# Clustered attention and a gated FFN on one core: masks of the last pairs written by VectorE, raw weights loaded two chunks ahead, results stored by quarters

## The chip, the cores and the metric

The kernel runs on one NeuronCore of a Trainium2 chip. The time is the device time of one execution in microseconds (us). Beside it stands the span of a profiled execution, which is what the views of the profile add up to.

## What is computed

Attention within clusters, for 4 batches, 8 heads, 768 tokens and 64 features, followed by a two-layer network with a hard-swish gate. Cut to what matters:

```python
q_assign = np.argmax(np.einsum('bhsd,hcd->bhsc', q_n, c_n), axis=-1)   # 16 clusters
k_assign = np.argmax(np.einsum('bhsd,hcd->bhsc', k_n, c_n), axis=-1)
mask = q_assign[:, :, :, None] == k_assign[:, :, None, :]
scores = np.where(mask, scale * np.matmul(q, k.transpose(0, 1, 3, 2)), -1e9)
attn = softmax(scores);  attn_out = np.matmul(attn, v)
x = attn_out.transpose(0, 2, 1, 3).reshape(3072, 512)
h = x @ w_in                          # 512 x 2048
g = h * np.clip(h + 3.0, 0.0, 6.0) / 6.0
out = g @ w_out                       # 2048 x 512
```

The weights w_in and w_out arrive as 64-bit floats, so the kernel has to make 32-bit floats of them itself.

## The kernel before, in words

**Steps.** Two heads are worked on together as a pair; there are 16 pairs. A pair has 12 steps (two halves of 384 queries, six chunks of 128 keys), so there are 192 steps, numbered n, and r = n mod 12 is the place in the pair. In a step, `scores` computes the scores of both heads into a PSUM tile `ps` (two such tiles exist), `exponentials` has ScalarE write exp of them into `ex`, `key_sums` has GpSimd add `ex` to a running sum `acc`, and `attn_v` multiplies `ex` by v into `pv`. When a half is done, `divide` multiplies `acc` by ones on TensorE (`pd`), VectorE takes the reciprocal `rcp` and multiplies it into `num`, and `num` is stored to a scratch tensor `xd` in DRAM.

**The mask.** A score of different clusters must vanish. `route` finds each token's cluster as a one-hot row; `route_turn` transposes the rows on TensorE (`po`) and ScalarE copies them to `xm`, scaled by -2^60 for keys (whose one-hot is inverted). In `scores_part`, a bf16 product of `xm` adds -2^60 to the scores of unlike clusters, and an f32 product of `xf` (the transposed q and k) adds the scores. The names `MASKED`, `by_vector`, `masks`, `clusters` and `spread` belong to another way, in which VectorE masks `ex` with cluster numbers; with `MASKED = NPAIR` no pair uses it.

**Preparing a pair.** `prep_items` spreads the work for the next pair over the steps: `turn` (12 transpositions `pqk` of q and k, copied to `xf`), `cluster_scores` (`pcs`), `route`, `route_turn`.

**Weights.** `decoding_steps` gives five steps for each of 32 chunks of 64-bit weights (`raw`, two buffers): `split`, `join`, `power`, `rest`, `total`, on VectorE and ScalarE. `split` of chunk i also issues the load of chunk i+1. `share` says how many of these steps follow each pair of scores steps. After the chunks, `weight_sums` and `make_first_sums` form sums of weights on VectorE.

**The network.** It is computed by a scheme with seven products in place of eight (half-size blocks, sums before and after). A block of 256 tokens is 15 items: eight `up` (products `uX`, `uY`, VectorE's sums `sx` and `g_sb`, ScalarE's `lift`, VectorE's `clip`, GpSimd's gated sums) and seven parts of `down` (products `X` and `Y`, sums into `y0` and `y1`). There are twelve blocks. `psum_m`, two banks, holds the outputs of both.

**Order.** The order on every engine is written out by hand in the recording loop; each engine runs its instructions in that order, and semaphores hold one that depends on another engine. Up to step 96 (`DECODED`) steps come two at a time. From there `four_by_four` groups them: at r mod 4 = 0 a block of scores, then `attn_v` of four steps; at r mod 4 = 2 a block of scores and after it the fill, some four items of the network with the next pair's preparation between them. After step 192 only the network is left. Nearly all DMAs are issued by SyncE (SP), which too waits in order.

**Lines of the profile.** L418 is the scores product (`ps`), L441 exp, L461 and L464 `acc`, L474 `pv`, L495 `pd`, L499 and L500 `rcp` and `num`, L310 `pqk`, L323 `pcs`, L367 `po`, L208 the load of raw weights, L221 to L252 the decoding, L658 and L669 the up products and sums, L693 and L700 the down products and sums, L740 and L742 the stores of results.

Of the kernel before, what the change touches and what calls it, by code (L numbers as in the profile page):

```python
# [116 lines left out]
def fast_path(ctx, tc, ok, q, k, v, centroids, moe_w_in, moe_w_out, out):  # L117
# [26 lines left out]
    rawp = decoding.enter_context(tc.tile_pool(name="rawp", bufs=2))  # L144
# [24 lines left out]
    MASKED = NPAIR  # L169
# [40 lines left out]
    def decoding_steps(i):  # L210

        got = {}

        def split():
            load_weights(i + 1)
            raw = st.pop(("raw", i))
            got.update(lo=raw[:, :, 0], hi=raw[:, :, 1])
            got["size"] = decp.tile([P, WC], BF16, name="wsize")
            got["top"] = psum_t.tile([P, WC], U32, name="wtop", tag="t")
            got["unit"] = decp.tile([P, WC], U32, name="wunit")  # L220
            nc.scalar.activation(  # L221
                out=got["size"], in_=got["hi"].bitcast(F32), func=ACT.Abs,
                accum_out=w_totals[:, 0, i : i + 1],
            )
            nc.vector.tensor_scalar(
                out=got["top"], in0=got["hi"], scalar1=3, scalar2=0x3FFFFFFF,
                op0=ALU.logical_shift_left, op1=ALU.bitwise_and,
            )

        def join():  # L230
            nc.vector.scalar_tensor_tensor(
                out=got["top"], in0=got["hi"], scalar=0xC0000000, in1=got["top"],
                op0=ALU.bitwise_and, op1=ALU.bitwise_or,
            )

        def power():
            nc.scalar.activation(
                out=got["size"], in_=got["size"], func=ACT.Relu, bias=w_low, scale=-1.0,
                accum_out=w_totals[:, 1, i : i + 1],
            )  # L240
            nc.vector.tensor_scalar(
                out=got["unit"], in0=got["top"], scalar1=0xFF800000, scalar2=None, op0=ALU.bitwise_and
            )

        def rest():
            unit = got["unit"].bitcast(F32)
            nc.vector.scalar_tensor_tensor(
                out=unit, in0=got["lo"], scalar=2.0**-52, in1=unit, op0=ALU.mult, op1=ALU.mult
            )

        def total():
            nc.vector.tensor_tensor(  # L252
                out=chunks[i][0], in0=got["top"].bitcast(F32), in1=got["unit"].bitcast(F32), op=ALU.add
            )

        return [split, join, power, rest, total]
# [6 lines left out]
    number = const.tile([P, C], BF16, name="number")  # L263

    def constants():
        make_identity(nc, ident)
        for t in range(2):
            nc.vector.tensor_reduce(
                out=parity[:, t : t + 1],
                in_=ident.rearrange("p (h t c) -> p t h c", t=2, c=C)[:, t], axis=AX.XY, op=ALU.max,  # L270
            )
        nc.gpsimd.memset(half_c, 0.5)
        nc.gpsimd.memset(low_c, 1.0 / BOUND)
        nc.gpsimd.memset(ones, 1.0)
        nc.gpsimd.memset(w_low, W_LOW)
        nc.gpsimd.memset(one_hot, 0.0)
        for c in range(C):
            nc.gpsimd.memset(number[:, c : c + 1], float(c))

        warm = psum_t.tile([P, 4, P], F32, name="warm", tag="t")  # L280
        for i in range(14):
            nc.tensor.transpose(out=warm[:, i % 4], in_=ident, identity=ident)
# [11 lines left out]
    def centroid_turn():  # L294
        pc = scratch([P, P], "pc")
        nc.tensor.transpose(out=pc, in_=st.pop("wide"), identity=ident)
        nc.vector.tensor_copy(out=cnT, in_=pc)
# [5 lines left out]
    def turn(g, part):  # L303
# [4 lines left out]
        for i in range(4):  # L308
            j = part * 4 + i
            nc.tensor.transpose(out=pt[:, i], in_=qk[:, j // NCH, j % NCH], identity=ident)  # L310
        dst = xf[:, part * 4 : part * 4 + 4]
        nc.scalar.copy(out=dst, in_=pt)
# [17 lines left out]
    def route(g):  # L330
# [27 lines left out]
        if g >= MASKED:  # L358
            numbers.append(lambda: clusters(g))

    def route_turn(g, part):
# [7 lines left out]
        nc.scalar.activation(out=dst, in_=po, func=ACT.Copy, scale=-FAR if part else 1.0)  # L369
# [6 lines left out]
    def clusters(g):  # L376
        oh = one_hot.rearrange("p j (t c) -> p j t c", t=2)[:, :, :, 0:C]
        which = rtp.tile([P, NC2, 2, C], BF16, name="which")
        nc.vector.tensor_tensor(
            out=which, in0=oh, in1=number.unsqueeze(1).unsqueeze(1).to_broadcast([P, NC2, 2, C]), op=ALU.mult  # L380
        )
        qid = st["qid"] = rtp.tile([P, NCH, 2], BF16, name="qid")
        kid = st["kid", g] = kidp.tile([P, NCH, 2], F32, name="kid")
        nc.vector.tensor_reduce(out=kid, in_=which[:, NCH:], axis=AX.X, op=ALU.add)

        nc.vector.tensor_scalar(
            out=kid, in0=kid, scalar1=-1.0, scalar2=C * (C - 1) / 2.0, op0=ALU.mult, op1=ALU.add
        )
        qsum = rtp.tile([P, NCH, 2], F32, name="qsum")
        nc.vector.tensor_reduce(out=qsum, in_=which[:, 0:NCH], axis=AX.X, op=ALU.add)  # L390
        nc.vector.tensor_copy(out=qid, in_=qsum)

    def spread(g, part):
        if part == 0:
            st["xm", g] = xp.tile([P, NC2, P], BF16, name="xm")
        pb = scratch([P, 4, P], "pb")
        for i in range(4):
            t, j = divmod(4 * part + i, NCH)
            nc.tensor.matmul(
                pb[:, i], lhsT=st["qid"][:, j, t : t + 1].to_broadcast([P, P]), rhs=ident_q,  # L400
                start=True, stop=True,
            )
        nc.scalar.copy(out=st["xm", g][:, 4 * part : 4 * part + 4], in_=pb)
# [6 lines left out]
    def scores_qk(n):  # L410
        st["ps", n] = psum_s.tile([P, 2, 512], F32, name="ps")
        scores_part(n, st["xf", where(n)[0]], True, by_vector(n))

    def scores_part(n, x, first, last):
        g, hf, j = where(n)
        for t in range(2):
# [3 lines left out]
                rhs=x[r, hf * NHC : (hf + 1) * NHC], start=first, stop=last,  # L420
            )
# [3 lines left out]
    def scores(n):  # L425
        g, hf, j = where(n)
        if ("ps", n) not in st:
            if hf == j == 0 or by_vector(n):
# [6 lines left out]
        if not by_vector(n):  # L435
            scores_part(n, st["xm", g], False, True)
# [6 lines left out]
    def masks(n):  # L443
        g, hf, j = where(n)
        if not by_vector(n):
            return
        ex = st["ex", n]
        for t in range(2):
            nc.vector.scalar_tensor_tensor(
                out=ex[:, t].rearrange("p (a b) -> p a b", b=P),  # L450
                in0=st["xm", g][:, t * NCH + hf * NHC : t * NCH + (hf + 1) * NHC],
                scalar=st["kid", g][:, j, t : t + 1], in1=ex[:, t].rearrange("p (a b) -> p a b", b=P),
                op0=ALU.is_equal, op1=ALU.mult,
# [32 lines left out]
    def divide(n):  # L486
        g, hf, _ = where(n)
# [10 lines left out]
        rcp = nump.tile([P, HALF], F32, name="rcp")  # L498
        nc.vector.reciprocal(out=rcp, in_=pd)  # L499
        nc.vector.tensor_tensor(out=num, in0=num, in1=rcp, op=ALU.mult)  # L500

        def keep():
            nc.sync.dma_start(st["xd", b][:, kt, hf * HALF : (hf + 1) * HALF], num)
            in_range(2 * g + hf, rcp)
            if (kt, hf) == (NKT - 1, 1):
                later.append(lambda: (waiting.extend((b, m) for m in range(NHC)), load_block()))

        return keep
# [93 lines left out]
    def ffn_items(b):  # L602
# [99 lines left out]
        def down(m, part):  # L702
            def item():
# [29 lines left out]
                elif part == 3:  # L733
                    add(y1[:, 0:HC], y0[:, HC:], st["Y"][:, HC:])
                    add(y1[:, HC:], y1[:, 0:HC], st["Y"][:, 0:HC])
                elif part == 4:
                    nc.scalar.copy(out=y0[:, 0:HC], in_=st["X"][:, 0:HC])
                elif part == 6:
                    add(y1[:, 0:HC], y0[:, HC:], st["Y"][:, HC:])
                    nc.sync.dma_start(out_v[b, 2 * m + 1], y1)  # L740
                    add(y0[:, HC:], y0[:, HC:], st["Y"][:, 0:HC])
                    nc.sync.dma_start(out_v[b, 2 * m], y0)  # L742
# [42 lines left out]
    def prep_items(g, r, fours):  # L785
# [5 lines left out]
        if g >= MASKED:  # L791
            one_hots = [lambda part=part: spread(g, part) for part in range(3)]
# [22 lines left out]
    def share(n, r):  # L815

        if n < READY:
            return {0: 4, 2: 2, 4: 3, 6: 1, 8: 2, 10: 4}[r]
        return {0: 6, 2: 5, 4: 5, 6: 3, 8: 5, 10: 5}[r]
# [10 lines left out]
    fill, checks, unmasked = [], [], []  # L830
# [11 lines left out]
    def four_by_four(n, r, steps):  # L842
        for i in steps:
            scores(i)
        if r % 4 == 2:
            for i in steps:
                exponentials(i)
            unmasked.extend(steps)
            check_all()
            for op in numbers:  # L850
                op()
            numbers.clear()
# [6 lines left out]
        for i in unmasked:  # L859
            masks(i)  # L860
            key_sums(i)
        unmasked.clear()
        if r == 4 or n >= total:
            m = n - r % per_pair - 1 if n < total else total - 1
            if ("acc", *where(m)[:2]) in st and m < st["valued"]:
                later.append(divide(m))
                ready(m)
        for i in range(st["valued"], min(n, total)):
            attn_v(i)
            if i % per_pair == NCH - 1:  # L870
                later.append(divide(i))
        st["valued"] = min(n, total)
        for i in steps[1 if r == 8 else 2 :]:
            exponentials(i)
        for i in steps:
            masks(i)
            key_sums(i)

    with tc.manual_schedule():
# [8 lines left out]
        centroid_turn()  # L888
        nc.vector.tensor_copy(out=ident_q, in_=ident)
        load(1, "q", "k")  # L890
        cluster_scores(0)
# [6 lines left out]
        for n in range(0, total + lag_d + 2, 2):  # L898
# [25 lines left out]
            if not fours or r % 4 == 2 or n >= total:  # L924
                want = min(items_by(n + 2) - st["done"], len(fill))
                st["done"] += want
                for i in range(max(len(prep), want)):
                    if i < want:
                        fill.pop(0)()
                    if i < len(prep):  # L930
                        prep[i]()
            if r == 6 and fours:
# [386 lines left out]
```

## Time and profile before

| | |
|---|---|
| three runs | 1012.68, 1014.41, 1016.15 us; median 1014.41 |
| profiled run | 1013.51 us, span 1011.7 us, TensorE clock 0.999 |
| decoding of the weights | VectorE's L225 from 12.1 to 227.8 us |
| steps 120 to 191 | 378 to 783 us of the span |
| network alone | from 783 us to the last product at 1005.3 us |

How to read it: the page gives each engine's busy time and its share of the span. A row of the groups names line, engine, operation, output and inputs, shapes and count, then busy time and the mean of one, then the idle time of the engine ahead of it and what ended that. Waits are summed by who waited for whom. Where two products overlap in TensorE's pipeline, the mean of one is longer than what one adds to the stream; the starts in the timeline tell that.

### The profile page before, as it was taken

How to read it: one execution, taken by the hardware profiler on the slowest of the kernel's cores; microseconds unless marked ns; L12 is line 12 of the kernel's file. 1: busy time of each engine (PE TensorE's matmuls, PEld its weight loads, DVE VectorE, ACT ScalarE, POOL GpSimd, SP SyncE). 2: the span in 40 equal slices, each digit the busy share in tenths (PEclk: the TensorE clock that was granted, in tenths of full speed). 3: DMA queues.
4: the chain of work that ended last, by engine and by line, in shares of the span. 5: the costliest groups of instructions: out<-in, count | busy, mean ns of one | idle time of the engine just before them, and what ended most of it. 6: DMA issues, size and time to landing. Idle time of an engine off the chain costs nothing.

```text
span 1011.7 us, 16735 instructions
## 1 busy us (share of the span) xinstructions
PE 988.1 (98%) x6560; PEld 734.7 (73%) x6560; DVE 564.5 (56%) x1085; ACT 390.3 (39%) x764; POOL 430.8 (43%) x363
## 2 busy tenths in 40 slices
PE   8999989999999999999999999999999999999997
PEld 4444445555688777788787777778787898999996
DVE  4888888988954255226336237137146372727270
ACT  6788877666233233234323333333223120202010
POOL 4778756665416326426415416515526130303030
PEclk9999999999999999999999999999999999999999
DMA  7344455432253052222323224123033051414120
GB/s 184 102 117 135 125 162 146 139 105 71 102 169 84 9 147 76 55 78 86 75 84 97 51 69 131 32 76 102 22 91 92 22 149 34 139 40 128 51 64 25
DMA packets 87560, 92.70 MB, mean 92 GB/s; under 512 B 53936, under 2 KB 68272, under 8 KB 87472
## 3 DMA queue, kind: packets, MB, share of 16 engines
q1 hardware_dynamic: 87328, 91.51, 31.8%
q8 instruction: 54, 0.88, 0.4%
q14 instruction: 34, 0.28, 0.1%
q10 hardware_dynamic: 144, 0.03, 0.0%
HBM read 75.79 MB, written 15.73 MB: 90 GB/s over the span
## 4 chain that ended last, share of the span: by engine, by line
PE 87%; DVE 6%; ACT 4%; DMA 1%; issue 1%; SPq 0%; ACTq 0%; DVEq 0%
PE Y L693 16%; PE uY L658 15%; PE ps L418 13%; PE X L693 12%; PE uX L658 12%; PE pv L474 11%; PE pd L495 2%; PE pqk L310 2%; PE ph L613 2%; DVE tx L580 1%; PE pcs L323 1%; DMA raw<-in_moe_w_out_dram 1%; ACT ex L441 1%; PE po L367 1%; DVE rcp L499 1%
## 5 line engine op out<-in xcount | busy, mean ns | idle before, releaser
L464 POOL TENSOR_TENSOR acc<-acc,ex 128x768 f32<-128x768 f32 x128 | 241.8, 1889 | 130.7 <-ACT ex L441 124.0
L648 POOL TENSOR_TENSOR g_sb<-g_sb 128x256 f32<-128x256 f32 x176 | 127.5, 746 | 319.2 <-DVE g_sb L526 297.9
L441 ACT ACTIVATE ex<-ps 128x768 f32<-128x768 f32 x192 | 148.4, 805 | 85.1 <-PE ps L418 84.5
L523 ACT ACTIVATE sx<-g_sb,half_c 128x512 f32<-128x512 f32 x88 | 63.5, 722 | 268.2 <-DVE g_sb L669 268.2
L418 PE MATMUL ps<-xf 64*128 64x384 f32 x768 | 157.0, 487 | 0.8 <-ACT ex L441 0.8
L474 PE MATMUL pv<-ex,vt 128*64 128x384 f32 x768 | 141.1, 496 | 0.0
L700 DVE TENSOR_TENSOR y<-y,Y 128x256 f32<-128x256 f32 x48 | 20.2, 421 | 169.9 <-PE Y L693 169.1
L474 PEld LDWEIGHTS pv<-ex,vt 128*64 128x64 f32 x768 | 48.7, 136 | 82.4 <-issue 72.7
L499 DVE RECIPROCAL rcp<-pd 128x384 f32<-128x384 f32 x32 | 81.8, 2557 | 47.6 <-PE pd L495 46.7
L461 POOL TENSOR_TENSOR acc<-ex 128x768 f32<-128x768 f32 x32 | 59.6, 1864 | 101.2 <-ACT ex L441 101.1
L658 PE MATMUL uX<-xb,w_in_sb 128*128 128x128 f32 x704 | 93.0, 275 | 0.0
L693 PE MATMUL X<-w_out_sb,g_sb 128*128 128x256 f32 x384 | 89.7, 381 | 0.0
L693 PE MATMUL Y<-T,g_sb 128*128 128x256 f32 x384 | 87.3, 380 | 0.0
L693 PE MATMUL Y<-w_out_sb,g_sb 128*128 128x256 f32 x384 | 87.2, 380 | 0.0
L658 PEld LDWEIGHTS uX<-xb,w_in_sb 128*128 128x128 f32 x704 | 85.7, 192 | 0.0
L418 PEld LDWEIGHTS ps<-xf 64*128 64x128 f32 x768 | 67.7, 188 | 21.7 <-issue 18.0
L693 PEld LDWEIGHTS X<-w_out_sb,g_sb 128*128 128x128 f32 x384 | 71.2, 190 | 12.9 <-issue 3.5
L693 PEld LDWEIGHTS Y<-T,g_sb 128*128 128x128 f32 x384 | 72.3, 190 | 11.2 <-issue 1.7
L693 PEld LDWEIGHTS Y<-w_out_sb,g_sb 128*128 128x128 f32 x384 | 72.2, 190 | 11.1 <-issue 1.1
L526 DVE SCALAR_TENSOR_TENSOR g_sb<-sx,g_sb 128x512 f32<-128x512 f32 x88 | 67.3, 770 | 1.0 <-ACT sx L523 0.9
L418 PE MATMUL ps<-xm 64*128 64x384 bf16 x384 | 61.0, 327 | 6.5 <-ACT ex L441 3.4
L669 DVE TENSOR_TENSOR g_sb<-uY,sx 128x128 f32<-128x128 f32 (+1 forms) x176 | 65.6, 414 | 0.1
(110 smaller groups left out, 1380.3 us busy)
## 6 DMA issues: line engine op xcount, KB each, us to landing
tx<-td SPq DMA_DIRECT2D x86, 384.0 KB, 3.2
raw<-in_moe_w_in_dram SPq DMA_DIRECT2D x16, 512.0 KB, 4.0
raw<-in_moe_w_out_dram SPq DMA_DIRECT2D x16, 512.0 KB, 3.6
qk<-in_q_dram SPq DMA_DIRECT2D x32, 192.0 KB, 4.5
qk<-in_k_dram SPq DMA_DIRECT2D x32, 192.0 KB, 4.6
vt<-in_v_dram SPq DMA_DIRECT2D x32, 192.0 KB, 3.8
xd<-num SPq DMA_DIRECT2D x32, 192.0 KB, 2.9
xb<-xd SPq DMA_DIRECT2D x12, 512.0 KB, 4.2
```

The source lines that it names most:

```text
L418: nc.tensor.matmul(st["ps", n][:, t, 0:HALF], lhsT=x[r, NCH + j], rhs=x[r, hf * NHC : (hf + 1) * NHC], start=first, stop=last,)
L441: nc.scalar.activation(out=ex, in_=sc, func=ACT.Exp, scale=SM_SCALE)
L461: nc.gpsimd.tensor_tensor(out=acc, in0=st["ex", n - 1], in1=ex, op=ALU.add)
L464: nc.gpsimd.tensor_tensor(out=acc, in0=acc, in1=ex, op=ALU.add)
L474: nc.tensor.matmul(pv[t * D : (t + 1) * D], lhsT=vt[:, t, j], rhs=ex[:, t], start=(j == 0), stop=(j == NCH - 1),)
L499: nc.vector.reciprocal(out=rcp, in_=pd)
L523: nc.scalar.activation(out=r, in_=h, func=ACT.Relu, bias=half_c, scale=1.0 / 6.0)
L526: nc.vector.scalar_tensor_tensor(out=g, in0=r, scalar=1.0, in1=h, op0=ALU.min, op1=ALU.mult)
L648: eng.tensor_tensor(out=out_, in0=in0, in1=in1, op=op)
L658: nc.tensor.matmul(dst, lhsT=w[:, kt], rhs=x(kt), start=(kt == 0), stop=(kt == HK - 1))
L669: nc.vector.tensor_tensor(out=out_, in0=in0, in1=in1, op=ALU.add)
L693: nc.tensor.matmul(bank[:, half * HC : (half + 1) * HC], lhsT=g_sb[:, kind, i], rhs=w[:, i], start=(first and i == 0), stop=(last and i == ...
```

## The change

1. `raw` gets a third buffer, and `split` of chunk i issues the load of chunk i+2. The shares of decoding steps change by one at r = 2 (3 for 2, before step 56) and at r = 4 (4 for 5, after).
2. Pairs 10 to 15 (steps 120 to 191) are masked by VectorE, and in another place: ahead of the scores product, `masks` writes -2^60 or 0 into the PSUM tile, by comparing query numbers in `xm` with a key's number, and the f32 product is added onto it. The masks of step n+2 follow the exponentials of step n; those for the next block at r mod 4 = 0 are spread through the fill, one head at a time. `clusters` becomes three small steps at the end of a fill, and `spread` makes 12 bf16 transpositions.
3. `key_sums` follows the exponentials at once at r mod 4 = 2. `pd` of a half now stands behind its last `attn_v` (`sum_up`), at r = 0 and 8, and `rcp` and `num` stand at the end of that block.
4. At the start, five idle transpositions and the centroids' transposition come between those of q and those of k, and VectorE makes one of three copies to `xf` and one of two to `xm`.
5. Results are stored by quarters, as they come; in the last four blocks of the network ScalarE issues the last of the four.

```diff
-    rawp = decoding.enter_context(tc.tile_pool(name="rawp", bufs=2))
+    rawp = decoding.enter_context(tc.tile_pool(name="rawp", bufs=3))
...
-    MASKED = NPAIR
+    MASKED = NPAIR // 2 + 2
...
         def split():
-            load_weights(i + 1)
+            load_weights(i + 2)
...
+            if g == 0 and j == NCH:
+
+                idle(5)
+                centroid_turn()
             nc.tensor.transpose(out=pt[:, i], in_=qk[:, j // NCH, j % NCH], identity=ident)
...
+        if g == 0 and part == 2:
+            nc.vector.tensor_copy(out=dst, in_=pt)
+        else:
+            nc.scalar.copy(out=dst, in_=pt)
...
+        pb = scratch([P, NCH, P], "pb", BF16)
+        for j in range(NCH):
+            nc.tensor.transpose(
+                out=pb[:, j], in_=st["qid"][:, j, t : t + 1].to_broadcast([P, P]), identity=ident_q
+            )
+        nc.scalar.copy(out=st["xm", g][:, t * NCH : (t + 1) * NCH], in_=pb)
...
+        if by_vector(n):
+
+            scores_part(n, st["xf", g], False, True, True)
+            return
...
-        for t in range(2):
-            nc.vector.scalar_tensor_tensor(
-                out=ex[:, t].rearrange("p (a b) -> p a b", b=P),
+        if ("ps", n) not in st:
+            st["ps", n] = psum_s.tile([P, 2, 512], F32, name="ps")
+        for t in heads:
+            nc.vector.tensor_scalar(
+                out=st["ps", n][:, t, 0:HALF].rearrange("p (a b) -> p a b", b=P),
                 in0=st["xm", g][:, t * NCH + hf * NHC : t * NCH + (hf + 1) * NHC],
-                scalar=st["kid", g][:, j, t : t + 1], in1=ex[:, t].rearrange("p (a b) -> p a b", b=P),
-                op0=ALU.is_equal, op1=ALU.mult,
+                scalar1=st["kid", g][:, 1, j, t : t + 1], scalar2=-FAR,
+                op0=ALU.not_equal, op1=ALU.mult,
             )
...
                 elif part == 3:
                     add(y1[:, 0:HC], y0[:, HC:], st["Y"][:, HC:])
                     add(y1[:, HC:], y1[:, 0:HC], st["Y"][:, 0:HC])
+                    keep(1, 1, y1[:, HC:])
                 elif part == 4:
                     nc.scalar.copy(out=y0[:, 0:HC], in_=st["X"][:, 0:HC])
+                    keep(0, 0, y0[:, 0:HC])
                 elif part == 6:
                     add(y1[:, 0:HC], y0[:, HC:], st["Y"][:, HC:])
-                    nc.sync.dma_start(out_v[b, 2 * m + 1], y1)
+                    keep(1, 0, y1[:, 0:HC])
                     add(y0[:, HC:], y0[:, HC:], st["Y"][:, 0:HC])
-                    nc.sync.dma_start(out_v[b, 2 * m], y0)
+
+                    keep(0, 1, y0[:, HC:], nc.scalar if st["last"] else nc.sync)
...
-            return {0: 4, 2: 2, 4: 3, 6: 1, 8: 2, 10: 4}[r]
-        return {0: 6, 2: 5, 4: 5, 6: 3, 8: 5, 10: 5}[r]
+            return {0: 4, 2: 3, 4: 3, 6: 1, 8: 2, 10: 4}[r]
+        return {0: 6, 2: 5, 4: 4, 6: 3, 8: 5, 10: 5}[r]
...
-            unmasked.extend(steps)
+            for i in steps:
+                key_sums(i)
             check_all()
...
+            for t in range(2):
+                singles.extend(lambda i=i, t=t: masks(i, [t]) for i in (n + 2, n + 3))
             return
...
+        for i in steps[: 1 if r == 8 else 2]:
+            masks(i + 2)
...
-            if i % per_pair == NCH - 1:
-                later.append(divide(i))
+            if i % NCH == NCH - 1 and i != DECODED - 1:
+                inverse = sum_up(i)
+                ready(i)
...
+        if inverse:
+            later.append(inverse())
```

## The prediction

> **What bounds the kernel now.** I read the page's part 1 first, then busy time by stage, then the waits of TensorE, then the timeline of one scores block. Part 1:
>
> ```profile
> span 1011.7 us, 16735 instructions
> PE 988.1 (98%) x6560; PEld 734.7 (73%) x6560; DVE 564.5 (56%) x1085; ACT 390.3 (39%) x764; POOL 430.8 (43%) x363
> ```
>
> TensorE (PE) stands still for only 1011.7 - 988.1 = 23.6 us. A gain must shorten its stream or come out of those 23.6 us. Where they lie, by stage (start:end, length, then busy us of each engine):
>
> ```profile
> core 0: us, PE busy (x) PEld busy (x) DVE busy (x) ACT busy (x) POOL busy (x), PEclk, DMA share, GB/s
> 0.00:25.00 25.00, 20.21 (x136) 11.32 (x138) 10.60 (x29) 16.97 (x33) 10.10 (x32) 1.00 0.70 182
> ...
> 100.00:290.00 190.00, 178.97 (x1095) 104.10 (x1095) 161.33 (x204) 118.92 (x257) 111.93 (x68) 1.00 0.44 126
> ...
> 378.00:783.00 405.00, 403.90 (x2759) 311.60 (x2757) 181.05 (x397) 132.92 (x237) 176.19 (x153) 1.00 0.27 76
> ...
> 1005.30:1011.70 6.40, 0.00 (x0) 0.00 (x0) 0.84 (x2) 0.00 (x0) 0.00 (x0) 0.77 0.25 90
> ```
>
> Idle PE: 4.8 us at the start, 11.0 us between 100 and 290 (weights are decoded there, VectorE is 85% busy), 6.4 us after the last product. In 378 to 783, steps 120 to 191, which is where the masks move, PE idles 1.1 us and VectorE is 45% busy. What PE waits for, over the whole run (total, times, longest), and the one engine held by a weight transfer:
>
> ```profile
> PE ps L418 <- ACT ex L441: 4.1, 6, 2.0
> PE pqk L310 <- ACT xf L312: 2.7, 2, 1.9
> PE pcs L323 <- DVE rcp L499: 2.5, 1, 2.5
> ...
> ACT wsize L221 <- DMA raw<-in_moe_w_out_dram: 7.9, 2, 5.0
> ```
>
> One scores block in the timeline (start, duration):
>
> ```profile
> 602.20 0.34 PE L418 MATMUL ps<-xm 64*128 64x384 bf16 x2
> 602.37 0.81 PE L418 MATMUL ps<-xf 64*128 64x384 f32 x4
> 603.02 0.33 PE L418 MATMUL ps<-xm 64*128 64x384 bf16 x2
> 603.18 0.81 PE L418 MATMUL ps<-xf 64*128 64x384 f32 x4
> 603.92 0.87 PE L495 MATMUL pd<-acc,ones 128*64 128x384 f32 x4
> ```
>
> Starts matter here, not durations: the mask product (ps<-xm) puts the next start off by 0.17 us, the f32 product by 0.65.
>
> **What the Trainium skill says.** "Trainium Kernel Development and Optimization", Performance Expectations, calls matmul busy time a bad metric because matmuls are pipelined. The trace agrees: 384 mask records of 327 ns mean would be 125 us, their busy time is 61 us, and the starts give 192 x 0.17 = 33 us; I use starts. "VectorE: DVE Perf Modes", Why PSUM operands drop a tier, leaves f32 with a PSUM operand at one element per cycle; its errata section prices PSUM to SBUF at 120 + FD cycles at 0.96 GHz, by which I estimate (120 + 384)/0.96 = 525 ns for a 384-wide mask (it prices no SBUF to PSUM). "SBUF — State Buffer", Who interferes with whom: a VectorE instruction with two SBUF inputs contends with GpSimd, one with a single SBUF input outside the two-port modes doesn't. The trace agrees on the first half (num of L500 takes 0.56 to 1.74 us). The new mask has one SBUF tensor. "DMA: Bandwidth & Descriptors", Issuing engines are not separate DMA queues: a second issuing engine only saves issue time.
>
> **The change, part by part.**
>
> *Masks off TensorE.* Pairs 10 to 15, 72 steps, lose their xm products. Two steps with masks run 602.20 to 603.92, 1.72 us; without, 2 x 0.65 + 0.09 for the change to the next kind = 1.39. That is 0.33 per two steps, 36 x 0.33 = 11.9; the six blocks that start a pair (1.81 us now) give 0.09 more each: **-12.4 us** on the path. The twelve transpositions per pair stay (six po in 0.33 us; six pb of bf16, by the nearest row the same). They read a column repeated 128 times: 0 taken, at worst 0.1 us each if such a load is not quick, 72 x 0.1 = 7 us.
>
> *Masks onto VectorE.* 144 tensor_scalar, bf16 in, f32 to PSUM, 128x384. No row shows it. Nearest: L225, tensor_scalar into PSUM, 695 ns for 512; 384-wide sums from PSUM 548 ns; so 0.55 us each (from the page's 0.525 up to 0.70), 79 us in all. Clusters adds 1.3 us per pair. VectorE's load in 378:783 goes from 181 to some 268 us of 405. The sum fits; its order decides. A step's chain becomes: exp of n on ScalarE frees the bank, two masks (1.1 us), then the scores of n+2. Behind a waiting mask stand the reciprocal and the sx sums of the next up unit; for those, PE waits by its two psum_m banks.
>
> (a) Block r=4: last up product at 602.2, exps at 603.98 and 604.7 (behind lift), masks of n+2 done 605.95, of n+3 at 607.1. PE: scores 1.4, pv 2.65, so n+2 starts at 606.3 and n+3 at 606.95: 0.2 us wait, six times, 1.2. (b) Block r=8: the second exp ends at 631.27 behind seen and num, its masks at about 632.9; PE asks at 632.45. Where the fill before ends in up units (three times), 0.5: 1.5. (c) Fill r=6 of up units: an up unit takes PE 3.13 us and VectorE 1.95 + 0.7 for clip = 2.65. Two masks make it 3.75, twice in a row, besides route's 1.17; waits of 0.2 and 0.5, pairs 13 to 15: 2.1. (d) The reciprocal of r=0 now starts behind four masks, 2.56 + num up to 1.7 us, ahead of the first unit's sums: 0.4 x 3 = 1.2. (e) Fill r=10: 0.3. Sum **+6.3 us**; from 1 (if sums overlap, as 0.62 us for two of 0.29 and the slack of 0.85 before uY sums suggest) to 14 (masks of 0.7).
>
> *key_sums earlier, pd after pv.* GpSimd's acc now stands ahead of the fill's gated sums: two of 1.9 us, done before the first clip of the fill (PE reaches X's second half 1.9 us after its s2). 0, hidden by up products; up to +2 by contention with clip.
>
> *Third raw buffer, shares.* Each load is issued one chunk (some 5 us of VectorE) ahead of now; landing takes 3.7 us, 7.6 at most. That covers ScalarE's two waits (5.0 and 2.9 us), which reached PE as 1.9 us (pqk <- xf, at 141) and 2.0 (ps <- ex, at 229): **-3.9 us**. Bounds 0 (VectorE at 85% is itself the limit, and the 2.5 us behind rcp at 270 stays) and -6. On SP the load waits for the same buffer as before (wunit of chunk i-1), so nothing queues longer. The shifted shares move ScalarE and VectorE work by one step, hidden under scores.
>
> *Start.* Five idle transpositions (0.16 to 0.23 us each) and pc stand ahead of k's transpositions; k lands at 6.71, the queue is free near 7.2: +0.5. VectorE's copies beside ScalarE save about 0.5 at xf and 0.3 at xm (13.98 now). **0**, from -0.8 to +0.7. Sixteen more memsets of GpSimd (0.6 us) end long before its first acc at 16.0.
>
> *Stores by quarters.* The final two stores hold 512 KB and land 3.5 us after issue; afterwards two of 128 KB, one issued by ScalarE at the same time. Half the bytes at the 370 GB/s seen there is 0.7 us, the issue some 0.1: **-0.8** (-0.3 to -1.2). Elsewhere SP issues 20 stores more, 0.34 us each. Stores of parts 3 and 4 wait for y sums in front of xd stores, tx and qk loads; those loads run two units or a pair ahead, and all stood behind part 6's stores anyway: 0.
>
> Sum: -12.4 + 6.3 - 3.9 + 0 - 0.8 = -10.8 us against the profiled span of 1011.7. That run was 1013.51, the three others 1012.68 to 1016.15, median 1014.41; 1014.4 - 10.8 gives **1003.5 us**.
>
> **Rivals.** *Masks hidden whole*: VectorE's slack (55%) takes them, 1 us of waits: 998.3. For it: 1.7 us of VectorE idle per unit at the r=2 fills. Against: at r=6 only 0.8 idle. *Little comes through*: waits of 10, raw gain 0: 1014.4 - 12.4 + 10 - 0.8 = 1011. For it: VectorE works without a gap from 236 to 276. *VectorE becomes the bound, slower*: in its fixed order the masks hold the sx sums in the 18 fills between steps. At 0.95 us a mask, four masks and two units take 9.1 us of VectorE against 6.3 of PE: about 2.3 us lost in nine fills of up units, 0.8 in twelve scores blocks, 31 us: 1014.4 - 12.4 - 4.7 + 31 = 1028. It turns at 17 us of waits, 0.95 per fill, a mask of about 0.8 us. Against: the rows above.
>
> **How the numbers follow.** Main case 0.52 (999 to 1008), hidden masks 0.23, little 0.12, slower 0.10, rest 0.03. Range 995 to 1011: main, hidden, half of the third. A measurement can tell about 0.3%, 3 us: faster is below 1011.4. Faster 0.52 + 0.23 + 0.07 = 0.82, same 0.06, slower 0.12.
>
> **What would show it.** Right: ps<-xm products gone from steps 120 on, busy PE shorter by some 12 us, masks of 0.5 to 0.6 us, PE waiting for VectorE (masks or sx) 4 to 8 us in the moved stage, ScalarE's wait for raw gone, the tail below 6 us. Wrong: masks over 0.8 us, PE idle in that stage over 15 us, pb transpositions slower than po, or the idle in 100 to 290 staying at 11 us.

## The result, and the profile after

The changed kernel takes 1007.53 us (median; 1006.22 to 1009.46), the kernel before 1014.02 in the same comparison. The ratio is 0.9936, 95% interval 0.9909 to 0.9962: about 6.5 us, or 0.6%, faster, 4 us slower than the forecast of 1003.5. The profiled execution is the slowest of the four, 1009.46 us with a span of 1007.6; the spans of the others were 1004.3, 1004.4 and 1007.0. Its page, part 1:

```profile
span 1007.6 us, 16709 instructions
PE 987.3 (98%) x6421; PEld 731.7 (73%) x6421; DVE 659.3 (65%) x1255; ACT 389.5 (39%) x762; POOL 431.7 (43%) x379
```

The mask products of 72 steps are gone (139 PE records fewer: 144 products less, five idle transpositions more) and VectorE works 95 us more, yet TensorE's busy time is only 0.8 us shorter, not 12. Busy time by stage, columns as in the prediction:

```profile
core 0: us, PE busy (x) PEld busy (x) DVE busy (x) ACT busy (x) POOL busy (x), PEclk, DMA share, GB/s
100.00:290.00 190.00, 182.31 (x1102) 104.48 (x1100) 163.18 (x203) 118.89 (x255) 113.28 (x69) 0.99 0.42 122
...
378.00:783.00 405.00, 402.59 (x2632) 308.39 (x2629) 264.63 (x558) 133.51 (x238) 176.86 (x154) 1.00 0.27 77
```

Between 100 and 290 us TensorE idles 7.7 us (11.0 before), and there is a new figure, a granted clock of 0.99. Where the masks went, VectorE is 65% busy and TensorE idles 2.4 us (1.1 before). The new masks, from the groups of VectorE (busy, mean ns, idle time ahead):

```profile
L472 DVE TENSOR_SCALAR ps<-xm,kid 128x384 f32<-128x384 bf16 x144 | 83.7, 616 | 26.4 <-ACT ex L463 23.2 <-ACT xm L421 1.8
```

They take 616 ns, where 550 was taken, and mostly wait for an exponential to free the bank. TensorE's waits over the whole run begin so:

```profile
PE po L379 <- DVE rcp L527: 2.2, 2, 1.8
PE ps L436 <- ACT ex L463: 1.6, 4, 0.6
PE pqk L318 <- ACT xf L324: 1.6, 2, 0.8
PE uX L688 <- DVE sx L699: 1.4, 7, 0.4
```

Gone are the 2.5 us of pcs behind the reciprocal and the 2.0 us of ps behind an exp; new are 2.2 us of po behind a reciprocal, 1.8 of them in one wait. Waits for the masks are hardly to be seen here: `ps <- DVE ps` has 0.3 us in all. The transpositions pb are no slower than po.

Neither view says where the 12 us of the forecast are. The starts do. I took the start of each `pv` block in the trace of before, and how much earlier or later the same block starts in the others (us; minus is ahead of before). Besides before and after, the runs are those told below:

```
before    after   old start  masks on PE  no masks  old shares  raw only
 101.6    +1.1      +0.1        -0.5        -0.4       -0.5       +0.2
 145.3     0.0      -1.0        -1.6        -1.4       -1.6       -0.9
 185.6    +1.0       0.0        -0.6        -0.4       -1.6       -0.9
 232.6    -1.1      -2.1        -2.6        -2.5       -3.7       -3.0
 244.5    +1.4      -0.4        -0.9        -0.8       -3.7       -3.0
 265.4    +2.3      -0.4        -0.9        -0.8       -3.7       -3.0
 288.9    -0.3      -3.0        -3.5        -3.4       -6.3       -5.5
 358.9    -0.3      -3.0        -3.5        -3.4       -6.3       -5.5
 781.9    -3.5      -6.1        -3.8       -12.2       -9.3       -5.6
```

In "after" the row of 265.4 stands 2.7 us behind "old start", although the work from 100 us on is the same in both. That is this one execution: 1.0 us comes from its start, 1.65 from a fall of the clock behind the 1.8 us wait (both below). With 0.5 us won in the tail, the last row's 3.5 makes the 4.1 by which the spans differ (1011.7 to 1007.6, but for rounding).

The last product ends at 1001.70 us (1005.27 before), and the span 5.9 us later (6.4 before).

### The profile page after: what moved, and what is told of

The parts are those of the page before. It is cut to its first block, busy times and chain, and to the rows that moved or that the text cites. A ratio compares the mean times of both kernels' runs of the same rounds, so it can differ in the third digit from the quotient of the medians.

```text
span 1007.6 us, 16709 instructions
## 1 busy us (share of the span) xinstructions
PE 987.3 (98%) x6421; PEld 731.7 (73%) x6421; DVE 659.3 (65%) x1255; ACT 389.5 (39%) x762; POOL 431.7 (43%) x379
## 4 chain that ended last, share of the span: by engine, by line
PE 73%; DVE 5%; ACT 1%; issue 1%; ACTq 0%; DVEq 0%
PE Y L723 17%; PE uY L688 14%; PE X L723 12%; PE uX L688 11%; PE ps L436 8%; PE pv L497 7%; PE pqk L318 1%; PE pd L521 1%; DVE sx L699 1%; PE ph L643 1%; DVE g_sb L699 1%; PE pcs L335 1%; DVE g_sb L556 1%; DVE ps L472 1%; DVE T L577 1%
## 5 line engine op out<-in xcount | busy, mean ns | idle before, releaser
L472 DVE TENSOR_SCALAR ps<-xm,kid 128x384 f32<-128x384 bf16 x144 | 83.7, 616 | 26.4 <-ACT ex L463 23.2
L556 DVE SCALAR_TENSOR_TENSOR g_sb<-sx,g_sb 128x512 f32<-128x512 f32 x88 | 64.4, 735 | 1.6 <-ACT sx L553 1.6
```

The lines of the kernel that those rows point to most:

```text
L472: nc.vector.tensor_scalar(out=st["ps", n][:, t, 0:HALF].rearrange("p (a b) -> p a b", b=P), in0=st["xm", g][:, t * NCH + hf * NHC : t * NC ...
L556: nc.vector.scalar_tensor_tensor(out=g, in0=r, scalar=1.0, in1=h, op0=ALU.min, op1=ALU.mult)
```

## The experiments

Every ratio is to the kernel before, timed on the same chip.

### The start of before

```diff
             if g == 0 and j == NCH:
-                idle(5)
-                centroid_turn()
...
+        centroid_turn()
```

with ScalarE's copies restored as well.

> The changed kernel with the start of before (no five idle transpositions, the centroids' transposition behind those of k, ScalarE makes all copies to xf and xm). Theory: the new start puts k's transpositions behind 1.6 us of other work, and delays every step by 1.0 us (first masked product 15.04 us after, 14.04 before). Then that product starts near 14.0 again and the kernel is 1.0 us faster than the changed one: ratio to before near 0.9926. Rival: the late start came from q landing 0.27 us later in that one execution and from a TensorE that was slow by chance; then the ratio stays near 0.9936.

Measured: 1007.77 us, ratio 0.9939 (0.9921 to 0.9957). The interval holds both ratios expected, 0.9926 and 0.9936, so the times don't decide. The traces do, for the rival: the profiled start of the changed kernel was an unlucky one. Its TensorE, after waiting 0.67 us for q:

```profile
5.28 1.51 PE L318 MATMUL pqk<-ident,qk 128*128 128x128 f32 x6 [0.67 <-DMA qk<-in_q_dram]
6.58 1.27 PE L286 MATMUL warm<-ident 128*128 128x128 f32 x5
7.91 0.48 PE L300 MATMUL pc<-ident,cenwide 128*128 128x128 f32 x1
8.18 1.19 PE L318 MATMUL pqk<-ident,qk 128*128 128x128 f32 x6
```

Each transposition takes 0.25 us here up to some 8 us, where six took 0.96 us before (0.16 each). In the run with masks on PE the same rows read 0.85, 0.71 (five), 0.33 and 0.84. Over all traces with the new start, the first masked product began at 13.36 to 13.83 us in eight and at 15.04 and 15.41 in two; with the old start at 14.03, 14.04 and 14.25. So the new start usually gains 0.2 to 0.7 us and can lose 1.0 or more.

What made the two late ones late is in the traces as well. They keep the times at which the granted clock changed, which no view prints (the views count the time ahead of the first record as 1.00). The first record of full clock begins at 8.93 us in the changed kernel and at 9.34 us in the other late one, and at 4.42 to 6.36 us in the eleven others. In the changed kernel transpositions start 0.21 us apart up to that record and 0.11 us apart behind it. The two late executions also had the longest waits for q (0.67 and 1.00 us, at most 0.61 in the others); whether that is the reason no run shows.

### The masks left on TensorE, and no masks at all

```diff
-    MASKED = NPAIR // 2 + 2
+    MASKED = NPAIR
```

> The changed kernel with MASKED = NPAIR: the masks of all pairs stay on TensorE, all other parts kept. Theory: the moved masks bring 3.2 us net in steps 120 to 191 (from the starts of corresponding blocks: 0.33 us ahead of before at step 120, 3.49 ahead at 191), so the kernel is 3.2 us slower than the changed one, ratio to before near 0.9968, and no step from 120 on is ahead by more than at 120. Rival, the prediction's sum: 6.1 us net, ratio near 0.9996.

Measured: 1011.5 us, ratio 0.9971 (0.9957 to 0.9985), and from step 120 to 191 it gains 0.3 us on before. The move of the masks is worth some 3 us net, half of the 6.1 forecast.

```diff
-            scores_part(n, st["xf", g], False, True, True)
+            st["ps", n] = psum_s.tile([P, 2, 512], F32, name="ps")
+            scores_part(n, st["xf", g], True, True)
...
-        if n >= total or not by_vector(n):
+        if True:
             return
```

> The changed kernel, in which pairs 10 to 15 are not masked at all, by no engine (that part of the computation is left out; cluster numbers and their copies are still made). It gives the gain that would come without any wait for VectorE's masks. Theory: a scores block of two steps takes 1.49 us without mask products, since each mask product of 0.17 us hid 0.09 us of loading the weights of the f32 product, so 30 blocks give 0.23 and six give 0.32, 8.8 us in all: 5.6 us faster than the changed kernel, ratio near 0.9881, all blocks 1.49. Rival, the prediction's price (blocks of 1.39, 12.4 us): ratio near 0.9845.

Measured: 1000.33 us, ratio 0.9855 (0.9838 to 0.9872), between the two ratios expected. The shortest span is 998.5 us, 5.8 below the shortest of the changed kernel, where the theory said 5.6. The trace decides: from 358.9 to 781.9 it gains 8.8 us on before (-3.4 to -12.2), as the theory said, and TensorE waits 0.5 us for VectorE in that stage. A block of it, with the start of the next kind of product behind it:

```profile
594.41 1.56 PE L436 MATMUL ps<-xf 64*128 64x384 f32 x8
595.90 2.48 PE L498 MATMUL pv<-ex,vt 128*64 128x384 f32 x14
```

1.49 us for two steps, not 1.39. So the masks' products were worth 8.8 us, and the changed kernel, which gains 3.0 to 3.2 in that stage, spends 5.6 to 5.8 on waiting for VectorE.

### The third raw buffer, taken away and alone

```diff
-    rawp = decoding.enter_context(tc.tile_pool(name="rawp", bufs=3))
+    rawp = decoding.enter_context(tc.tile_pool(name="rawp", bufs=2))
...
-            load_weights(i + 2)
+            load_weights(i + 1)
```

> The changed kernel with two raw buffers and loads one chunk ahead, as before (the new shares kept). Theory: the third buffer takes away ScalarE's waits for raw (7.9 us, 3.0 of them reaching TensorE in the traces), but VectorE, 85% busy there, gives most of it back as waits behind the reciprocal, so it is worth 1.4 us: ratio near 0.9950, ScalarE's two raw waits back. Rival, the prediction's sum: worth 3.9, ratio near 0.9974. Second rival: worth nothing, 0.9936.

Measured: 1008.26 us, ratio 0.9935 (0.9917 to 0.9953). The interval holds 0.9936 and the theory's 0.9950 and leaves out the prediction's 0.9974. Of ScalarE's two raw waits one is back (2.9 us), and TensorE's start at 145 is 1.0 us later than with three buffers, but the waits at 229 and 270 us stay gone. By the starts the buffer is worth some 1 us inside the changed kernel, then. The opposite edit, three buffers alone in the kernel before, with the same lines the other way round:

> The kernel before with one part of the change alone: three raw buffers, loads two chunks ahead. Theory: only one of the two waits that the prediction gave to raw is its own (pqk behind xf at 141, 1.0 us shorter in all kernels with three buffers and not in the one with two); the other (ps behind ex at 229, 2.0) goes with the changed shares, for it was gone with two buffers too. So 1.0 us faster than before, ratio 0.9990, the 2.0 at 229 and the 2.5 behind the reciprocal at 270 still there. Rival, the prediction's sum: both go, 3.9 us, ratio 0.9962.

Measured: 1009.37 us, ratio 0.9955 (0.9937 to 0.9972). My theory fell: alone the buffer shortens the first of three waits by 1.1 us (1.9 to 0.8) and takes away the other two, 2.0 and 2.6 us. That is 5.7 us by the starts, more than the rival's 3.9; the ratio, some 4.6 us, doesn't tell the two apart. TensorE's waits between 100 and 290 us in it, where before had 4.1, 2.7 and 2.5 (pcs behind rcp):

```profile
PE ps L418 <- ACT ex L441: 2.2, 5, 0.6
PE pqk L310 <- ACT xf L312: 1.6, 2, 0.8
PE ps L418 <- ACT xm L369: 1.6, 4, 0.5
```

The third of these waits, pcs behind the reciprocal, hung on more than late data. Around that reciprocal, in the kernel before and then with the buffer alone:

```profile
264.79 2.38 DVE L580 TENSOR_TENSOR tx<-w_in_sb,tx 128x256 f32<-128x256 f32 x2
267.09 2.02 DVE L580 TENSOR_TENSOR w_in_sb<-w_in_sb 128x256 f32<-128x256 f32 x1
269.82 2.55 DVE L499 RECIPROCAL rcp<-pd 128x384 f32<-128x384 f32 x1
```

```profile
261.23 0.88 DVE L580 TENSOR_TENSOR tx<-w_in_sb,tx 128x256 f32<-128x256 f32 x2
262.03 0.42 DVE L580 TENSOR_TENSOR w_in_sb<-w_in_sb 128x256 f32<-128x256 f32 x1
263.15 2.55 DVE L499 RECIPROCAL rcp<-pd 128x384 f32<-128x384 f32 x1
```

The reciprocal starts 5.08 us behind the start of its pd before, and 1.36 us with the buffer. Of these 3.7 us, 3.1 are the same three sums, which in before stand beside GpSimd's `acc` (265.07 to 268.83) and took 2.38 and 2.02 us in place of 0.88 and 0.42; VectorE's queue was only 0.6 us later against TensorE. That `acc` is what slows the sums is my reading of these traces; no run takes it apart.

In the same stretch, 100 to 290 us, the changed kernel gains only 3.0 us, with this buffer in it. Something else takes 2.7 back.

### The shares of before

```diff
-            return {0: 4, 2: 3, 4: 3, 6: 1, 8: 2, 10: 4}[r]
-        return {0: 6, 2: 5, 4: 4, 6: 3, 8: 5, 10: 5}[r]
+            return {0: 4, 2: 2, 4: 3, 6: 1, 8: 2, 10: 4}[r]
+        return {0: 6, 2: 5, 4: 5, 6: 3, 8: 5, 10: 5}[r]
```

> The changed kernel with the shares of before (2 at r=2 up to step 56, 5 at r=4 after). Theory: the shares decide behind which decoding step and weight sum VectorE's reciprocals and ScalarE's exps stand between 178 and 275 us; with the old ones TensorE's 1.8 us behind the reciprocal at 241 goes, and the 2.0 at 229 and the 2.5 at 270 come back, about 2 us slower by the starts at step 120: ratio near 0.9956. Rival: the later place of pd, not the shares, took the 2.5 at 270 away; then the 270 wait stays gone and the kernel is as fast as the changed one or faster, 0.992 to 0.994.

Measured: 1004.7 us, ratio 0.9915 (0.9892 to 0.9937), in the rival's range, though not for its reason: the run before this one lost the wait at 270 without a later pd. What the shares do is seen on VectorE. The changed kernel, then the one with the old shares, around the reciprocal of the last half before step 96:

```profile
232.00 5.47 DVE L577 TENSOR_TENSOR T<-w_out_sb 128x1024 f32<-128x1024 f32 x2
237.40 2.83 DVE L577 TENSOR_TENSOR T<-w_out_sb,T 128x1024 f32<-128x1024 f32 x1
240.15 2.54 DVE L527 RECIPROCAL rcp<-pd 128x384 f32<-128x384 f32 x1
```

```profile
232.33 2.00 DVE L577 TENSOR_TENSOR T<-w_out_sb 128x1024 f32<-128x1024 f32 x1
234.25 2.54 DVE L527 RECIPROCAL rcp<-pd 128x384 f32<-128x384 f32 x1
```

The new shares take one decoding step more at r=2 in the five pairs before step 56, and one fewer at r=4 in the three pairs after it: by this reciprocal VectorE has been given two steps more, and these two are large sums of weights. It starts at 240.15 in place of 234.25, and the transpositions po, which need the bank that it reads, wait:

```profile
242.74 0.50 PE L379 MATMUL po<-ident_q,one_hot 128*128 128x128 bf16 x6 [1.84 <-DVE rcp L527]
```

With the old shares po follows ph at once (238.12 us, no wait). A second place, 1.0 us at 180 us (pqk behind rcp, with four steps more ahead of it), goes too. The starts say 2.7 us; the ratios say 2.1, with intervals that overlap.

### Every mask written twice

```diff
-        for t in heads:
+        for t in [t for t in heads for _ in range(2)]:
             nc.vector.tensor_scalar(
```

> The changed kernel with every mask of VectorE written twice (288 in place of 144, the same values), some 88 us more of VectorE in steps 120 to 191, which makes 350 of 405 us. Theory: what counts is the order on VectorE, not its share: four masks of 2.45 us more stand ahead of the scores at r=6 (2.8 us of wait each in six places), 1.2 to 2.4 at r=10 and r=2, and the sums of up units wait behind those spread in the fills: 25 to 40 us slower than the changed kernel, ratio 1.02 to 1.033. Rival: VectorE's free third of that stage takes them, below 5 us, ratio up to 0.9985.

Measured: 1078.4 us, ratio 1.0638 (1.0615 to 1.0661). The theory's kind is right and its size far too small: 71 us. The rival is out.

```profile
PE ps L436 <- DVE ps L472: 39.5, 32, 1.7
PE uX L688 <- DVE sx L699: 16.4, 21, 1.7
```

VectorE is busy for 348 of 465 us in the stage (75%) and holds TensorE up all the same, 32 times ahead of scores and 21 times in up units; the granted clock falls to 0.5 to 0.9 in stretches of 5 us behind some of these waits.

### The lift behind the exponentials

In the changed kernel, ScalarE and VectorE around the block at r=4 of pair 13:

```profile
601.02 0.72 ACT L553 ACTIVATE sx<-g_sb,half_c 128x512 f32<-128x512 f32 x1 [2.43 <-DVE g_sb L699]
601.65 1.49 ACT L463 ACTIVATE ex<-ps 128x768 f32<-128x768 f32 x2
```

```profile
602.48 2.45 DVE L472 TENSOR_SCALAR ps<-xm,kid 128x384 f32<-128x384 bf16 x4 [0.95 <-ACT ex L463]
```

```profile
604.09 1.90 PE L436 MATMUL ps<-xf 64*128 64x384 f32 x8
605.92 0.85 PE L335 MATMUL pcs<-xf,cnT 128*32 128x384 f32 x8
```

The scores were done by some 600.7 us, but the first exp starts at 601.65, behind a lift that waits for VectorE's sums. The four masks end at 604.93, and the next scores take 1.83 us instead of 1.49, with no idle time shown.

```diff
-            lift(sx, g)
+            late.append(lambda: lift(sx, g))
...
         for i in steps[: 1 if r == 8 else 2]:
             exponentials(i)
+        lifts()
```

> The changed kernel, in which ScalarE makes the lift of a fill's last up unit behind the exponentials of the next scores block, not ahead of them (its clip comes one unit later anyway). Theory: the first exp of a block waits 1.0 us for a lift that itself waits for VectorE's sums, and so the masks of the next steps end 0.3 us too late for the scores at r=6; then these six waits of 0.34 us go and those at r=10 shrink: 2 to 3 us faster than the changed kernel, ratio 0.9906 to 0.9916. Rival: VectorE's own queue binds the masks, no change, 0.9936.

In this first form the clip of the last unit of each block of tokens stood ahead of its own lift, so that unit's gate is another value. Measured: 1010.98 us, ratio 0.9971 (0.9959 to 0.9982), some 3.5 us slower than the changed kernel and far from both ratios expected. The trace shows why: two of the lifts now wait for GpSimd's gated sums of their own unit, and hold up what ScalarE has to do next.

```profile
629.24 0.72 ACT L553 ACTIVATE sx<-g_sb,half_c 128x512 f32<-128x512 f32 x1 [2.87 <-POOL g_sb L684]
630.70 0.46 ACT L503 COPY num<-pv 128x384 f32<-128x384 f32 x1
```

Behind this one a `pv` of TensorE waited 3.0 us for num, and behind the other, at 329.37 us, a `pqk` waited 1.9 us for xf; no later form shows either. The profiled execution also had the latest start of all (15.41 us) and two falls of the clock. Its blocks at r=6 all took 1.49 to 1.50 us, so the waits there do come from the lift; the time of this form doesn't say what that is worth.

### A version that beats both

The lift is made at once where the unit is the last of its block, and the old shares come back:

```diff
                 if i == HF - 1:
+                    lifts()
                     st.pop(("xb", b, m)), st.pop(("xs", b, m), None)
```

> The changed kernel with the shares of before, and with the lift of a fill's last up unit behind the exponentials of the next scores block (unless it is the last unit of a block of tokens). Theory: the two add up, for they act in different stages: no wait behind a reciprocal at 180 to 241 us (2.7 us, seen gone with the old shares), and no wait of 0.34 us in the scores at r=6 and r=10 (some 2.6 us over eight places, seen gone with the later lift): ratio 0.9885 to 0.9895. Rival: what is won at r=6 is given back in the fills, whose first clips come later: as with the old shares alone, 0.9915.

Measured: 1002.48 us (1002.29 to 1003.17), ratio 0.9885 (0.987 to 0.99). It is faster than both kernels, and in the range expected, though one of the two terms gave less than was counted on (below). The block above, now:

```profile
594.53 1.51 ACT L463 ACTIVATE ex<-ps 128x768 f32<-128x768 f32 x2 [2.30 <-PE ps L436]
595.93 0.72 ACT L553 ACTIVATE sx<-g_sb,half_c 128x512 f32<-128x512 f32 x1
```

```profile
597.73 1.56 PE L436 MATMUL ps<-xf 64*128 64x384 f32 x8
599.22 0.85 PE L335 MATMUL pcs<-xf,cnT 128*32 128x384 f32 x8
```

By the starts the masked stage gains 4.2 us (from -6.07 at 379 to -10.24 at 782) instead of 3.0; so the lift gives 1.2 us, half of what I expected, since the two waits at r=10 (0.33 and 0.58 us) didn't shrink, a third wait, of 0.5 us, came there, and the first block at r=6 kept its 0.34. The rest of the ratio comes from the shares, and from a clock that stands at 1.000 over the profiled run.

> As the run with old shares and later lifts, and pair 9 (steps 108 to 119) masked by VectorE too. Theory: VectorE is half idle from 290 us on, and the pair gives what the later ones give, five blocks of 0.23 and one of 0.32 less some waits: 1.0 us faster, ratio 0.001 lower. Rival: its cluster numbers fall into 270 to 290 us, where VectorE makes the weights' sums and works without a gap, and its masks wait behind those: no gain or slower by up to 2 us.

Measured: 1003.01 us, ratio 0.9891 (0.9873 to 0.9909): no gain that the times show. By the starts it is 0.6 us ahead of the run before it at 782; the difference is too small to be told from none.

### The stores of before

```diff
-                    keep(1, 1, y1[:, HC:])
...
-                    keep(0, 0, y0[:, 0:HC])
...
-                    keep(1, 0, y1[:, 0:HC])
+                    nc.sync.dma_start(out_v[b, 2 * m + 1], y1)
...
-                    keep(0, 1, y0[:, HC:], nc.scalar if st["last"] else nc.sync)
+                    nc.sync.dma_start(out_v[b, 2 * m], y0)
```

> The changed kernel with results stored as before (two stores of 256 KB at the end of each block of the network, both from SP). Theory: from the last product to the end of the span it takes 0.5 us longer than the changed kernel (5.9 us there, 6.4 before), 6.4 us. Rival, the prediction's 0.8 from half the bytes: 6.7 us. Second rival: the bytes don't matter, 5.9 us.

Measured: 1007.73 us in one execution. Its last product ends at 998.75 and the span at 1005.9, 7.2 us later. The two other traces with the old stores show 6.4 us (before) and 8.0 (raw only); the ten traces with quarters show 5.6 to 6.7, half of them below 6.0. By the middle values, 7.2 and 6.0, the quarters gain 1.2 us, but one execution can differ from the next by as much.

## Why the forecast was near, and which of its steps failed

The terms that missed, by size and by the experiment that measured them:

| step of the sum | forecast | measured | by |
|---|---|---|---|
| masks off TensorE | -12.4 | -8.8 | no masks at all |
| waits for VectorE's masks | +6.3 | +5.6 to +5.8 | that, against the stage of the changed kernel |
| third raw buffer | -3.9 | -5.7 alone, by the starts | raw only |
| shifted shares | 0 | +2.7 | old shares |
| start | 0 | mostly -0.2 to -0.7, twice +1.0 or more | all traces |
| quarters | -0.8 | about -1.2, -0.5 in this pair of traces | stores of before, all traces |

With -0.5 for the start and -0.5 for the stores, these make some -7.1 us, which from the span of 1011.7 is 1004.6; the two shortest spans of the changed kernel are 1004.3 and 1004.4. The profiled one has two accidents more: a start 1.5 us later than that -0.5, and 1.65 us of lowered clock. That the sum came within 4 us is in part luck: the raw buffer, the start and the waits turned out better than forecast by 3 us, the masks and the shares worse by 6.3. The term of `key_sums` and the later pd, forecast at nothing, holds: with old shares the changed kernel gains 5.74 us between 101.6 and 288.9, and the buffer alone 5.75; with masks on PE, all other parts together gain 0.3 from step 120 on.

*Masks off TensorE*, the largest miss, is a mis-sized term. The prediction took 0.65 us for an f32 product, the distance from its start to the next mask's, and charged 0.09 for "the change to the next kind" once per block. In the run without masks two f32 products of a block follow each other at 1.49 / 2 = 0.745 us: the 0.09 is due at every f32 product that isn't followed by a mask. The trace of before held the hint. Its second f32 product is followed by pd after 0.74 us, and the rows of weight loads show the weights of `xf` being loaded from 602.20 us on, along with the mask's product. That the load is what costs the 0.09 is my reading; no run takes it apart.

*The waits* were right in sum and, but for (d), in place. Against the run without masks, the changed kernel loses 1.6 us in the blocks at r=6 ((a), 1.2 forecast), 1.0 in those at r=10 ((b), 1.5), 2.1 in the fills of up units at r=6 ((c), 2.1), nothing behind the reciprocal of r=0 ((d), 1.2) and 0.9 in the fills at r=10 ((e), 0.3). The block at r=6 waits some 0.34 us (in four pairs of six, 0.28 in a fifth) in place of the 0.2 of (a); four masks of 616 ns in place of 550 are 0.26 us, enough for the difference (the estimate of 525 from the Trainium skill, "VectorE: DVE Perf Modes", errata section, was too low by 91 ns; it prices the other direction). But the sign that I named, 4 to 8 us of waits in the view, did not appear: the view shows 2.1 in that stage, 0.4 of them for ScalarE's num, and the starts 5.7. A wait inside a group of products counts as busy, as the block at 604.09 shows, 0.34 us longer with no idle time. For that reason "busy PE shorter by 12" failed as well.

*The raw buffer*: the prediction held the reciprocal's 2.5 us at 270 to be VectorE's own limit. The buffer alone removes it. Late data put VectorE back by 0.6 us of the 3.7; the other 3.1 are the three sums that then stood beside GpSimd's `acc`. So most of the 2.6 us won there hangs on which sums stand beside it, and that was not in the sum. And of the 1.9 us at 141 only 1.1 were late data.

*The shares* are the step that failed in kind: "hidden under scores" is wrong. In a stage where VectorE has hardly a gap, steps drawn forward move everything behind them, and two sums of 2 to 3 us came ahead of a reciprocal for which TensorE waits. The waits at 229 and 270 us are gone with the buffer alone, and gone as well in the changed kernel with two buffers. In the latter it may be the shares or another part of the change, the later pd for one; no run takes these two apart. With the buffer there, only the price of the shares is left.

The chain for VectorE as the bound was right in its place, and it doesn't need a full VectorE: with every mask written twice, and VectorE at 75%, it costs 71 us.

## What to carry to other kernels

Take what an instruction adds to the stream from two successors, the one it has now and the one it will have: removing a product brings less than its distance when it covered the start of the next. When busy time doesn't move, compare the starts of the same block in both traces; waits of a third of a microsecond inside a group of matmuls show in no other view. And where two edits aim at the same wait, try each alone: here one of them (the shares) only cost beside the other, and leaving it out gave nearly as much as the whole move of the masks.

## What the runs showed of the hardware

A mask of 128x384 from bf16 in SBUF to f32 in PSUM on VectorE took 605 to 623 ns, in all 144 cases.

The granted TensorE clock fell behind pauses of TensorE, but not each time. Behind the 1.8 us wait at 241 it stood at 0.94 and 0.71 in two stretches of 5 us in the changed kernel (0.90 and 0.76 in the run with two raw buffers), and `pv` of two steps took 2.46 us in place of 1.51. It fell there in the first form of the later lift too, and stayed at 1.0 in the five other runs with the same wait. In the traces' records each of these falls is one stretch of 3.41 us at half clock (244.45 to 247.86 in the changed kernel); with masks written twice some last 6.83. At the start of an execution the first record of full clock came between 4.42 and 9.34 us.

Three sums of 128x256 on VectorE took 1.3 us in all in one trace, and 4.4 in another, in which they stood beside GpSimd's `acc`.

Executions of one kernel differ by 3 to 4 us, often along with the clock: the run with the old start had spans of 1004.7 to 1005.2 us at clocks of 0.998 to 0.999 and 1006.8 to 1009.0 at 0.997. But the clock is not all of it: without the long waits, the version that beats both spread over 0.9 us only, while the run with pair 9 spread over 4.4 us, and its slowest execution stood at 1.000. What decides whether the clock falls, and what makes that other spread, stays open.
